# First taps of a pair's convolution, placed by an estimated landing time of their rows

## The chip, the cores and the metric

The kernel runs on one core of a Trainium2 chip. The metric is the device time of one execution in microseconds (us); the figure for the kernel before is the median of three runs.

## The reference

Two layers on `x` (8 batches, 4096 tokens, 192 channels). First a causal convolution over tokens with 7 taps; the taps are a softmax over the 7 weights of each of 8 heads, and a head has 24 channels. Then an MLP mixer:

```python
x_unf = x_pad[:, idx, :].reshape(B, S, K, H, group)
out = np.einsum('hk,bskhg->bshg', w, x_unf)          # the convolution
...
h = np.maximum(xt @ w_tok1, 0.0) @ w_tok2            # mixing of tokens
u = x + h.transpose(0, 2, 1)
h2 = np.maximum(u @ w_ch1, 0.0) @ w_ch2              # mixing of channels
return (u + h2).astype(np.float32)
```

## The kernel before, in words

**Groups and tiles.** The batches go in groups 0 to 4: two single batches (0 and 1), then three pairs (batches 2 and 3, 4 and 5, 6 and 7). The main loop goes over a group's 8 tiles of 512 tokens. Products keep float32's accuracy by splitting each operand into a high and a low part.

**One tile's steps on TensorE.** `mix2` (L899 to L901) finishes the token mixing. For a pair, DVE adds it to `u` (L914) and transposes it (L915), `blocks_sent` (L948) sends the blocks to their places with 16 small DMAs from SP and POOL, and `parted` makes the operands: `own_hi` on ACT (L961), `own_lo` on DVE (L963), and swapped copies in `other` (L966 on ACT, L968 by DMA). `channel1` is the first channel product (L999), in six steps of two results; from each result ACT makes `hh` (L1038) and DVE makes `hl` (L1039). `channel2` (L1073, L1074) and `channel2_halves` (L1056) are the second product, four parts `j` per tile; DVE adds each part's result into `osb` (L1079 and L1080, or L1062 and L1064). All results share `ps_x`, six PSUM buffers used in turn, so TensorE can be only a few results ahead of ACT and DVE.

**A turn.** In a pair's group, one `mix2` serves the tiles of both batches. It stands behind the second batch's `channel1`; that batch's `channel2` follows, with `parted` in its middle, and then `channel1` of the next tile's first batch. This text calls the place where that `channel1` begins a turn. The turns that matter here are in group 2: T1 begins at 607.00 us, T2 at 667.50, T3 at 735.80, T4 at 810.84 and T5 at 875.58 in the profiled execution.

**Work in the background.** While TensorE works on one group, a later group is convolved and its first token product is made (`stage1`). A pair is convolved in four blocks of 1024 tokens, q0 to q3 (`q2` in the code). For each half of the heads ("part") two DMAs on SP load the raw rows, 672 KB each (L639). The first tap of a head is a scaled copy on ACT (L649), which starts `xc`; the other six are multiply-adds on DVE into `xc` (L651). Finished blocks are stored to DRAM (`xcd`, L682, on POOL) and split for the product (`xhl`, ACT L734 and DVE L738).

**What sets the order.** The instructions are written out once, in Python, by a planner. `Background` keeps two running times in nanoseconds, `pe` and `dve`: what TensorE and DVE have been given so far. `fg` adds foreground work and then fills in background items while `dve` is not too far ahead of `pe`. An item can have a gate; a first tap's gate (`loaded`) is a time, and the tap is placed when `pe` has come to it. Each engine then runs its own instructions strictly in the order written, and waits in place for operands.

**Keeping loads back.** From before the `channel1` of a pair's second batch until `blocks_sent` is done, `bg.hold()` collects loads of raw rows and stores of `xcd`; `release` issues them right behind the 16 small DMAs. In the kernel before, a pair's load is marked, when it is issued, with `max(pe, dve)`; a first tap becomes due 6 us after that (10 us for q0).

Of the kernel before, what the change touches and what calls it, by code (L numbers as in the profile page):

```python
# [22 lines left out]
class Item:  # L23
# [6 lines left out]
    def __init__(self, fn, cost=0.0, lag=0.0, pe=0.0, gate=None, tag=None, eager=False):  # L30
        self.fn, self.cost, self.lag, self.pe, self.gate, self.tag = fn, cost, lag, pe, gate, tag
        self.eager = eager


class Background:
# [6 lines left out]
    def __init__(self):  # L42
        self.streams = []
        self.tiled = False
        self.pe = 0.0
        self.dve = 0.0
        self.held = None

    def transfer(self, fn):
        if self.held is None:  # L50
            fn()
        else:
            self.held.append(fn)
# [4 lines left out]

    def release(self):
        fns, self.held = self.held or [], None  # L60
        for fn in fns:
            fn()

    def add(self, items, lead=0.0, group=None):
        total = sum(it.cost for it in items) or 1.0
        self.streams.append(dict(items=items, total=total, done=0.0, free=self.pe, lead=lead, group=group))
# [65 lines left out]
def conv_mixer_kernel(ctx: ExitStack, tc: tile.TileContext, x, weight, w_tok1, w_tok2, w_ch1, w_ch2, out):  # L132
# [35 lines left out]
    bg = Background()  # L168
# [447 lines left out]
    def stage1(gi, pools):  # L616
        bs = GROUPS[gi]
        nb = len(bs)
# [11 lines left out]
        def load(q2, part):  # L630

            ds = slice(part * DH, (part + 1) * DH)
            raw = pools(part).tile([P, RB + HALO, nb, DH], F32, name=f"raw{part}")
            for i, b in enumerate(bs):

                at = (b * S + q2 * ST - HALO) * D + ds.start
                assert at >= 0
                src = bass.AP(tensor=x.tensor, offset=x.offset + at, ap=[[RB * D, P], [D, RB + HALO], [1, DH]])
                nc.sync.dma_start(out=raw[:, :, i, :], in_=src)  # L639
                if q2 == 0:  # L640
                    nc.gpsimd.memset(raw[0:1, 0:HALO, i, :], 0.0)
            return raw
# [13 lines left out]
        done = {}  # L656

        def mark(*key):
            done[key] = max(bg.pe, bg.dve)

        def begin(q2, part):
            def fn():
                states[q2]["raw", part] = load(q2, part)
                mark("load", q2, part)

            bg.transfer(fn)

# [92 lines left out]
        last_q = RB // MJ - 1  # L760
        def loaded(q2, part):
            at = done.get(("load", q2, part))
            return None if at is None or pools(q2 % 2) is None else at + (2e3 + 2e3 * nb if q2 else 10e3)

        def tap(q2, h, k):

            pace = PACE if gi == 1 and q2 + 1 < NS else 1.0
            it = Item(lambda: taps(q2, h, k), cost=2 * pace * (RB * nb * G / 0.96 + 130) if k else 0)
            if h % HH == 0 and k == 0:
                it.lag = 100  # L770

                def gate():
                    if h == 0 and q2 > 1 and ("split" if nb > 1 else "mixed", q2 - 2, last_q) not in done:
                        return None
                    return loaded(q2, h // HH)

                it.gate = gate
            convolving.append(it)
# [413 lines left out]
    for gi, bs in enumerate(GROUPS):  # L1192
        nb = len(bs)
# [109 lines left out]
```

## Time and profile before

| | us |
|---|---|
| median of 3 runs | 2048.83 (2048.3 to 2050.59) |
| the profiled execution's own time | 2047.31 |
| its span, first to last instruction | 2045.5 |
| TensorE busy | 2023.1 (99%) |
| DVE busy | 1453.1 (71%) |
| ACT, POOL busy | 761.7 (37%), 219.6 (11%) |

All readings below are of this one profiled execution. Its own time is 1.52 us under the median of the runs. In rows of the timeline, the first number is the start in us from the start of the span, the second the duration of the row's merged instructions; in brackets stands how long the engine was idle just before, and what ended that.

### The profile page before, as it was taken

How to read it: one execution, taken by the hardware profiler on the slowest of the kernel's cores; microseconds unless marked ns; L12 is line 12 of the kernel's file. 1: busy time of each engine (PE TensorE's matmuls, PEld its weight loads, DVE VectorE, ACT ScalarE, POOL GpSimd, SP SyncE). 2: the span in 40 equal slices, each digit the busy share in tenths (PEclk: the TensorE clock that was granted, in tenths of full speed). 3: DMA queues.
4: the chain of work that ended last, by engine and by line, in shares of the span. 5: the costliest groups of instructions: out<-in, count | busy, mean ns of one | idle time of the engine just before them, and what ended most of it. 6: DMA issues, size and time to landing. Idle time of an engine off the chain costs nothing.

```text
span 2045.5 us, 42015 instructions
## 1 busy us (share of the span) xinstructions
PE 2023.1 (99%) x17435; PEld 1858.9 (91%) x17435; DVE 1453.1 (71%) x2877; ACT 761.7 (37%) x1305; POOL 219.6 (11%) x383
## 2 busy tenths in 40 slices
PE   9999999999999989999999999999999999999999
PEld 9789999999988879999999999999999999999998
DVE  7899989999559978856985599545555555555554
ACT  4575534434332433333333334232323332333322
POOL 0100000000011011101111100111110011111110
PEclk9999999999999999999999999999999999999999
DMA  9845346554344475334645245533222333233310
GB/s 310 294 152 173 125 147 204 167 158 161 124 139 128 133 204 164 100 107 130 168 145 137 75 114 154 148 94 82 56 57 66 81 84 83 76 83 83 83 47 17
DMA packets 289230, 258.39 MB, mean 126 GB/s; under 512 B 209360, under 2 KB 238544, under 8 KB 289040
## 3 DMA queue, kind: packets, MB, share of 16 engines
q1 hardware_dynamic: 265120, 168.00, 28.9%
q0 software_dynamic: 23920, 87.71, 14.0%
q8 instruction: 138, 2.26, 0.5%
q14 instruction: 52, 0.43, 0.1%
HBM read 146.60 MB, written 71.30 MB: 107 GB/s over the span
## 4 chain that ended last, share of the span: by engine, by line
PE 89%; DVE 5%; DMA 3%; ACT 1%; SPq 1%; issue 0%; POOL 0%; ACTq 0%; POOLq 0%; DVEq 0%
PE ps_x L999 36%; PE ps_x L1073 16%; PE ps_x L1056 16%; PE ps_x L1074 7%; DVE xc L651 2%; PE ps_x L899 2%; PE ps_a L754 2%; PE ps_a L755 2%; PE ps_a L756 2%; PE ps_x L901 1%; PE ps_x L900 1%; DVE hl L1039 1%; DMA raw<-in_x_dram 1%; PE ps_a L444 1%; DMA dec_raw<-in_moe_w_tok_dram 1%; PE ps_x L896 1%
## 5 line engine op out<-in xcount | busy, mean ns | idle before, releaser
L1038 ACT ACTIVATE hh<-ps_x 128x512 fp32r<-128x512 f32 x756 | 410.6, 596 | 750.9 <-PE ps_x L999 750.9
L1039 DVE SCALAR_TENSOR_TENSOR hl<-ps_x,hh 128x512 fp32r<-128x512 f32 x756 | 484.3, 685 | 196.3 <-ACT hh L1038 195.3
L1073 PE MATMUL ps_x<-w,hh 128*128 128x384 f32 x1872 | 538.3, 359 | 0.1
L1074 PE MATMUL ps_x<-w,hl 128*128 128x192 f32 x1872 | 468.6, 250 | 0.0
L999 PE MATMUL ps_x<-other,w_hi 64*128 64x512 f32 x1728 | 452.7, 390 | 7.4 <-DVE osb L1080 7.2
L651 DVE SCALAR_TENSOR_TENSOR xc<-raw,cw,xc 128x384 f32<-128x384 f32 (+1 forms) x768 | 389.4, 561 | 24.7 <-ACT xc L649 24.7
L1074 PEld LDWEIGHTS ps_x<-w,hl 128*128 128x128 f32 x1872 | 357.4, 191 | 0.0
L999 PEld LDWEIGHTS ps_x<-other,w_hi 64*128 64x128 f32 x1728 | 314.7, 185 | 43.7 <-issue 8.3
L1073 PEld LDWEIGHTS ps_x<-w,hh 128*128 128x128 f32 x1872 | 351.5, 188 | 0.7 <-DVE hl L1039 0.7
L999 PE MATMUL ps_x<-own_hi,w_hi 64*128 64x512 f32 x1440 | 335.4, 394 | 5.7 <-DVE osb L1080 3.4
L1056 PE MATMUL ps_x<-w,hh 64*128 64x384 f32 x2304 | 330.2, 356 | 0.0
L999 PE MATMUL ps_x<-own_hi,w_lo 64*128 64x512 f32 x1440 | 326.2, 387 | 0.0
L999 PE MATMUL ps_x<-own_lo,w_hi 64*128 64x512 f32 x1440 | 326.1, 387 | 0.0
L1056 PE MATMUL ps_x<-w,hl 64*128 64x192 f32 x2304 | 291.7, 247 | 0.1
L999 PEld LDWEIGHTS ps_x<-own_hi,w_hi 64*128 64x128 f32 x1440 | 209.8, 184 | 40.5 <-issue 9.9
L999 PE MATMUL ps_x<-other,w_lo 64*128 64x512 f32 x864 | 242.8, 387 | 0.0
L999 PEld LDWEIGHTS ps_x<-own_hi,w_lo 64*128 64x128 f32 x1440 | 215.7, 184 | 27.5 <-DVE w_lo L204 0.5
L999 PEld LDWEIGHTS ps_x<-own_lo,w_hi 64*128 64x128 f32 x1440 | 215.8, 184 | 26.6
L1056 PEld LDWEIGHTS ps_x<-w,hl 64*128 64x128 f32 x2304 | 225.0, 188 | 1.8 <-DVE hl L1039 0.9
L1056 PEld LDWEIGHTS ps_x<-w,hh 64*128 64x128 f32 x2304 | 221.4, 184 | 0.9
L999 PEld LDWEIGHTS ps_x<-other,w_lo 64*128 64x128 f32 x864 | 159.4, 184 | 18.0
L1079 DVE TENSOR_TENSOR osb<-ps_x,u 128x192 f32<-128x192 f32 x156 | 55.4, 355 | 144.8 <-PE ps_x L1074 144.3
(143 smaller groups left out, 2151.6 us busy)
## 6 DMA issues: line engine op xcount, KB each, us to landing
raw<-in_x_dram SPq DMA_DIRECT2D x56, 672.0 KB, 7.2
t<-t2d SPq DMA_DIRECT2D x64, 512.0 KB, 5.4
out_dram<-osb POOLq DMA_DIRECT2D x63, 384.0 KB, 4.5
u<-xcd SPq DMA_DIRECT2D x62, 384.0 KB, 6.6
xcd<-xc POOLq DMA_DIRECT2D x28, 768.0 KB, 7.3
t<-t1p SPq DMA_DIRECT2D x32, 512.0 KB, 5.1
other<-own_hi SPq DMA_DIRECT2D x192, 48.0 KB, 2.1
other<-own_hi POOLq DMA_DIRECT2D x192, 48.0 KB, 2.0
```

The source lines that it names most:

```text
L651: nc.vector.scalar_tensor_tensor(out=dst, in0=src, scalar=cw[:, h, k:k + 1], in1=dst, op0=ALU.mult, op1=ALU.add)
L754: nc.tensor.matmul(out=ps, lhsT=wh, rhs=xh, start=a, stop=False)
L755: nc.tensor.matmul(out=ps, lhsT=wh, rhs=xl, start=False, stop=False)
L756: nc.tensor.matmul(out=ps, lhsT=wl, rhs=xh, start=False, stop=z)
L899: nc.tensor.matmul(out=ps[:, :n], lhsT=wh, rhs=hh, start=a, stop=False)
L999: nc.tensor.matmul(out=ps, lhsT=w1[w][rows, c, p * P:(p + 1) * P], rhs=t[h][v][rows, c], start=n == 0, stop=n == len(prods) - 1,)
L1038: nc.scalar.activation(out=h["hh", f], in_=ps, func=AF.Relu)
L1039: nc.vector.scalar_tensor_tensor(out=h["hl", f], in0=ps, scalar=0.0, in1=f32(h["hh", f]), op0=ALU.max, op1=ALU.subtract)
L1056: nc.tensor.matmul(out=ps[:, :m], lhsT=h[part, f][ks, ts], rhs=w2[ks, f, :m], start=n == 0 and part == "hh", stop=z and part == "hl",)
L1073: nc.tensor.matmul(out=ps[:, :2 * D], lhsT=h["hh", f][:, ts], rhs=w2[:, f, :], start=n == 0, stop=False)
L1074: nc.tensor.matmul(out=ps[:, :D], lhsT=h["hl", f][:, ts], rhs=w2[:, f, :D], start=False, stop=z)
L1079: nc.vector.tensor_tensor(out=rows(osb[:, j]), in0=rows(ps[:, :D]), in1=tokens(u, i)[:, j], op=ALU.add)
```

## The change

For a pair, a load no longer gets the time at which it is issued but an estimate of when it lands: 9 us after the later of now and the landing before it, so that loads are taken to land one by one. For loads that `release` issues, now is set 5 us later. The first tap is due at that estimate, with no further allowance. Single batches keep their rule.

```diff
@@ class Background
+        self.behind = 0.0
+        self.landing = 0.0
...
     def release(self):
         fns, self.held = self.held or [], None
+        self.behind = 5e3
         for fn in fns:
             fn()
+        self.behind = 0.0
+
+    def lands(self, took):
+        self.landing = max(max(self.pe, self.dve) + self.behind, self.landing) + took
+        return self.landing
@@ begin, in stage1
                 states[q2]["raw", part] = load(q2, part)
-                mark("load", q2, part)
+                if nb > 1:
+                    done["load", q2, part] = bg.lands(9e3)
+                else:
+                    mark("load", q2, part)
@@ loaded, in stage1
             at = done.get(("load", q2, part))
-            return None if at is None or pools(q2 % 2) is None else at + (2e3 + 2e3 * nb if q2 else 10e3)
+            if at is None or pools(q2 % 2) is None:
+                return None
+            return at if nb > 1 else at + (4e3 if q2 else 10e3)
```

No instruction is added or taken away on any engine; the same ones are written in another order. The order differs in two stretches only: a few taps of group 2 near 275 us, and the convolution of group 3 from T1 to T5 with what stands around it. From T5 on both orders are alike. In the changed kernel the line numbers are higher by 8 to 13 (L659 for L651, L976 for L963, L1092 and L1093 for L1079 and L1080, L1052 for L1039, L749 for L738, L657 for L649, L974 for L961, L979 for L966, L745 for L734, L1051 for L1038). Numbers behind names tell buffers apart.

DVE at T1, from `own_lo` to the first `hl`; `raw0_6694` holds the rows of block q0. Before:

```order
L963 TENSOR_TENSOR own_lo_6776<-other_6677,own_hi_6775 128x512 x3
L1079 TENSOR_TENSOR osb_6639<-ps_x_6758,u_6078 128x192
L1080 TENSOR_TENSOR osb_6639<-ps_x_6758,osb_6639 128x192
L651 SCALAR_TENSOR_TENSOR xc0_6822<-raw0_6694,cw_70,xc0_6822 128x16x24 x4
L1079 TENSOR_TENSOR osb_6639<-ps_x_6797,u_6078 128x192
L1080 TENSOR_TENSOR osb_6639<-ps_x_6797,osb_6639 128x192
L651 SCALAR_TENSOR_TENSOR xc0_6822<-raw0_6694,cw_70,xc0_6822 128x16x24 x4
L1039 SCALAR_TENSOR_TENSOR hl0_6841<-ps_x_6846,hh0_6840 128x512
```

Now:

```order
L976 TENSOR_TENSOR own_lo_6776<-other_6677,own_hi_6775 128x512 x3
L1092 TENSOR_TENSOR osb_6639<-ps_x_6758,u_6078 128x192
L1093 TENSOR_TENSOR osb_6639<-ps_x_6758,osb_6639 128x192
L1092 TENSOR_TENSOR osb_6639<-ps_x_6797,u_6078 128x192
L1093 TENSOR_TENSOR osb_6639<-ps_x_6797,osb_6639 128x192
L1052 SCALAR_TENSOR_TENSOR hl0_6834<-ps_x_6839,hh0_6833 128x512
L1052 SCALAR_TENSOR_TENSOR hl0_6834<-ps_x_6840,hh0_6833 128x512
L659 SCALAR_TENSOR_TENSOR xc0_6889<-raw0_6694,cw_70,xc0_6889 128x16x24 x2
```

The eight taps that stood ahead of the first `hl` stand behind it now, in twos.

DVE at T3, from `own_lo` to the first `hl`; before, `raw0_8260` holds the rows of block q2, loaded at this turn:

```order
L963 TENSOR_TENSOR own_lo_8354<-other_8243,own_hi_8353 128x512 x3
L651 SCALAR_TENSOR_TENSOR xc0_8387<-raw0_8260,cw_70,xc0_8387 128x16x24 x4
L1079 TENSOR_TENSOR osb_8171<-ps_x_8330,u_6835 128x192
L1080 TENSOR_TENSOR osb_8171<-ps_x_8330,osb_8171 128x192
L651 SCALAR_TENSOR_TENSOR xc0_8387<-raw0_8260,cw_70,xc0_8387 128x16x24 x8
L1079 TENSOR_TENSOR osb_8171<-ps_x_8396,u_6835 128x192
L1080 TENSOR_TENSOR osb_8171<-ps_x_8396,osb_8171 128x192
L738 TENSOR_TENSOR xhl_8433<-xc1_7597,xhl_8433 128x768
L651 SCALAR_TENSOR_TENSOR xc0_8387<-raw0_8260,cw_70,xc0_8387 128x16x24 x2
L1039 SCALAR_TENSOR_TENSOR hl0_8457<-ps_x_8462,hh0_8456 128x512
```

Now `raw1_7649` holds rows of block q1, long loaded, and `raw0_8252` those of q2:

```order
L659 SCALAR_TENSOR_TENSOR xc1_7680<-raw1_7649,cw_70,xc1_7680 128x16x24 x2
L976 TENSOR_TENSOR own_lo_8343<-other_8235,own_hi_8342 128x512 x3
L659 SCALAR_TENSOR_TENSOR xc1_7680<-raw1_7649,cw_70,xc1_7680 128x16x24 x2
L1092 TENSOR_TENSOR osb_8161<-ps_x_8322,u_6828 128x192
L1093 TENSOR_TENSOR osb_8161<-ps_x_8322,osb_8161 128x192
L659 SCALAR_TENSOR_TENSOR xc1_7680<-raw1_7649,cw_70,xc1_7680 128x16x24 x4
L1092 TENSOR_TENSOR osb_8161<-ps_x_8380,u_6828 128x192
L1093 TENSOR_TENSOR osb_8161<-ps_x_8380,osb_8161 128x192
L659 SCALAR_TENSOR_TENSOR xc0_8465<-raw0_8252,cw_70,xc0_8465 128x16x24 x6
L1052 SCALAR_TENSOR_TENSOR hl0_8438<-ps_x_8443,hh0_8437 128x512
```

All taps ahead of the last `osb` are of the old block; those of the new block begin behind it. On ACT, the four first taps of q2 stood right behind the swapped copies (L966); now the first `xhl` of q1 (L745) stands between.

DVE at T4, from `own_lo` to the first `hl`; before, `raw0_8767` (block q3, loaded 35 us earlier):

```order
L651 SCALAR_TENSOR_TENSOR xc1_9200<-raw0_8767,cw_70,xc1_9200 128x16x24 x6
L963 TENSOR_TENSOR own_lo_9212<-other_9087,own_hi_9211 128x512 x3
L651 SCALAR_TENSOR_TENSOR xc1_9200<-raw0_8767,cw_70,xc1_9200 128x16x24 x2
L1079 TENSOR_TENSOR osb_9015<-ps_x_9168,u_7610 128x192
L1080 TENSOR_TENSOR osb_9015<-ps_x_9168,osb_9015 128x192
L651 SCALAR_TENSOR_TENSOR xc1_9200<-raw0_8767,cw_70,xc1_9200 128x16x24 x4
L738 TENSOR_TENSOR xhl_9258<-xc0_8387,xhl_9258 128x768
L1079 TENSOR_TENSOR osb_9015<-ps_x_9249,u_7610 128x192
L1080 TENSOR_TENSOR osb_9015<-ps_x_9249,osb_9015 128x192
L651 SCALAR_TENSOR_TENSOR xc1_9200<-raw0_8767,cw_70,xc1_9200 128x16x24 x4
L1039 SCALAR_TENSOR_TENSOR hl0_9291<-ps_x_9296,hh0_9290 128x512
```

Now `raw1_8423` is of block q2, and `raw0_9091` of q3, loaded at this turn:

```order
L976 TENSOR_TENSOR own_lo_9180<-other_9074,own_hi_9179 128x512 x3
L659 SCALAR_TENSOR_TENSOR xc0_8465<-raw1_8423,cw_70,xc0_8465 128x16x24 x2
L1092 TENSOR_TENSOR osb_9002<-ps_x_9161,u_7592 128x192
L1093 TENSOR_TENSOR osb_9002<-ps_x_9161,osb_9002 128x192
L659 SCALAR_TENSOR_TENSOR xc1_9255<-raw0_9091,cw_70,xc1_9255 128x16x24 x10
L1092 TENSOR_TENSOR osb_9002<-ps_x_9217,u_7592 128x192
L1093 TENSOR_TENSOR osb_9002<-ps_x_9217,osb_9002 128x192
L749 TENSOR_TENSOR xhl_9253<-xc0_8465,xhl_9253 128x768
L659 SCALAR_TENSOR_TENSOR xc1_9255<-raw0_9091,cw_70,xc1_9255 128x16x24 x2
L1052 SCALAR_TENSOR_TENSOR hl0_9288<-ps_x_9293,hh0_9287 128x512
```

Ten taps of the block whose rows are loaded at this turn stand ahead of the last `osb`.

On SP, the loads of q1 and q3 for the first half of the heads, which went out between turns, go out at `release` now; the other halves' loads follow once their buffer is free. On POOL, the `xcd` stores of q1 and q2 stood ahead of the swapped copies (L968) at T3 and T4; they stand behind them now, and the store of q0 stands between the two output stores after T2 instead of ahead of both.

## The prediction

> **What bounds the kernel now.** I read the page's busy shares and chain first, then the waits of TensorE, then the timeline around them.
>
> ```profile
> PE 2023.1 (99%) x17435; PEld 1858.9 (91%) x17435; DVE 1453.1 (71%) x2877; ACT 761.7 (37%) x1305; POOL 219.6 (11%) x383
> ...
> PE 89%; DVE 5%; DMA 3%; ACT 1%; SPq 1%; issue 0%; POOL 0%; ACTq 0%; POOLq 0%; DVEq 0%
> ```
>
> TensorE bounds the kernel, and the change gives it no instruction less. So it can gain only time in which TensorE stands, or passes matmuls more slowly than elsewhere. The largest of its own waits:
>
> ```profile
> PE ps_x L999 <- DVE osb L1080: 10.5, 4, 4.4
> ```
>
> Four waits, 10.5 us: `channel1` needs a `ps_x` buffer that DVE has not emptied, since DVE is late with `osb`. They lie at T1, T2 and T3. Here stand, from the timeline, for T1 to T4 the first matmul of `channel1`, those that follow a wait, and the first of the product behind (L1056).
>
> ```profile
> 607.00 0.49 PE L999 MATMUL ps_x<-own_hi,w_hi 64*128 64x512 f32 x1
> 613.07 0.47 PE L999 MATMUL ps_x<-other,w_hi 64*128 64x512 f32 x1 [1.44 <-DVE osb L1080]
> 622.76 0.33 PE L1056 MATMUL ps_x<-w,hh 64*128 64x384 f32 x1
> 667.50 0.50 PE L999 MATMUL ps_x<-own_hi,w_hi 64*128 64x512 f32 x1
> 673.55 0.47 PE L999 MATMUL ps_x<-other,w_hi 64*128 64x512 f32 x1 [1.32 <-DVE osb L1080]
> 682.85 0.33 PE L1056 MATMUL ps_x<-w,hh 64*128 64x384 f32 x1
> 735.80 0.50 PE L999 MATMUL ps_x<-own_hi,w_hi 64*128 64x512 f32 x1
> 743.54 0.47 PE L999 MATMUL ps_x<-own_hi,w_hi 64*128 64x512 f32 x1 [3.36 <-DVE osb L1080]
> 748.43 0.76 PE L999 MATMUL ps_x<-other,w_hi 64*128 64x512 f32 x1 [4.42 <-DVE osb L1080]
> 758.27 0.33 PE L1056 MATMUL ps_x<-w,hh 64*128 64x384 f32 x1
> 810.84 0.49 PE L999 MATMUL ps_x<-own_hi,w_hi 64*128 64x512 f32 x1
> 823.24 0.33 PE L1056 MATMUL ps_x<-w,hh 64*128 64x384 f32 x2
> ```
>
> T4 is undisturbed: 823.24 - 810.84 = 12.40 us, 2.07 for each of six steps. T1 took 15.76, T2 15.35, T3 22.47: 3.36, 2.95 and 10.07 too much, **16.38 us** in all. Of it 10.54 is the four waits, 5.84 slow passing.
>
> Why DVE is late is seen on DVE, ACT and the DMAs: T1's and T2's row, then T3.
>
> ```profile
> 610.05 2.21 DVE L651 SCALAR_TENSOR_TENSOR xc<-raw,cw,xc 128x384 f32<-128x384 f32 x4 [4.27 <-ACT xc L649]
> ...
> 670.54 2.20 DVE L651 SCALAR_TENSOR_TENSOR xc<-raw,cw,xc 128x384 f32<-128x384 f32 x4 [2.75 <-ACT xc L649]
> ...
> 727.19 1.90 DVE L963 TENSOR_TENSOR own_lo<-other,own_hi 128x512 fp32r<-128x512 f32 x3 [0.46 <-ACT own_hi L961]
> 740.52 2.21 DVE L651 SCALAR_TENSOR_TENSOR xc<-raw,cw,xc 128x384 f32<-128x384 f32 x4 [11.44 <-ACT xc L649]
> 742.65 0.35 DVE L1079 TENSOR_TENSOR osb<-ps_x,u 128x192 f32<-128x192 f32 x1
> 743.03 0.36 DVE L1080 TENSOR_TENSOR osb<-ps_x,osb 128x192 f32<-128x192 f32 x1
> 743.31 4.31 DVE L651 SCALAR_TENSOR_TENSOR xc<-raw,cw,xc 128x384 f32<-128x384 f32 x8
> 747.54 0.35 DVE L1079 TENSOR_TENSOR osb<-ps_x,u 128x192 f32<-128x192 f32 x1
> 747.92 0.36 DVE L1080 TENSOR_TENSOR osb<-ps_x,osb 128x192 f32<-128x192 f32 x1
> 748.20 0.95 DVE L738 TENSOR_TENSOR xhl<-xc,xhl 128x768 fp32r<-128x768 f32 x1
> 749.06 1.14 DVE L651 SCALAR_TENSOR_TENSOR xc<-raw,cw,xc 128x384 f32<-128x384 f32 x2
> ```
>
> ```profile
> 724.94 14.45 SPq L639 DMA_DIRECT2D raw<-in_x_dram  x4
> 739.88 2.13 ACT L649 ACTIVATE xc<-raw,cw 128x384 f32<-128x384 f32 x4 [8.79 <-DMA raw<-in_x_dram]
> ```
>
> At T3 the rows are asked for at 724.94, behind the release; ACT stands until 739.88, and DVE, whose next taps need ACT's first one, for 11.44 us, with two parts of `osb` queued behind. From start to start four taps take 2.12 us (740.52 to 742.65) and two 1.06, so 0.53 each; `osb` takes 0.67, `xhl` 0.86. How long the second load of a part takes, beside the `xcd` stores at T3 and T4 and without them at T2:
>
> ```profile
> raw<-in_x_dram SPq DMA_DIRECT2D x1, 672.0 KB, 14.5
> xcd<-xc POOLq DMA_DIRECT2D x2, 768.0 KB, 8.4
> ...
> raw<-in_x_dram SPq DMA_DIRECT2D x1, 672.0 KB, 16.2
> ...
> raw<-in_x_dram SPq DMA_DIRECT2D x1, 672.0 KB, 7.4
> ```
>
> In order: T3, T4, T2.
>
> **The change part by part.** The measure for all turns is T4, where DVE was just early enough:
>
> ```profile
> 814.71 1.28 DVE L1039 SCALAR_TENSOR_TENSOR hl<-ps_x,hh 128x512 fp32r<-128x512 f32 x2
> 815.91 0.95 DVE L738 TENSOR_TENSOR xhl<-xc,xhl 128x768 fp32r<-128x768 f32 x1
> ```
>
> The first two `hl` took 1.20 and were done at 815.91, 5.1 us behind the turn. The six buffers go round: step 3 (2 x 2.07 = 4.1 us behind the turn) needs those of the last two parts `j`, step 4 (+6.2) those of step 1. So the last `osb` must be done by +4.1 and the first `hl` pair by +6.2.
>
> *T1.* No tap stands ahead of the first `hl`. Eight taps (4.24 us) and the 4.27 of waiting leave that place; `osb` is ready when TensorE is; step 1 ends at +2.1, and with 0.6 for `hh` and 1.20 the pair is done at about +4. Behind it taps and `hl` alternate at 1.06 + 1.20 = 2.26 us against 2.07: late by 0.19 a step, about 1 us over five steps, covered by the 2 us left. Gain 3.36 (at least the 1.44 of the wait).
>
> *T2.* Ahead of the first `hl` stand taps of the old block only, so no load is waited for.
>
> ```profile
> 665.23 1.90 DVE L963 TENSOR_TENSOR own_lo<-other,own_hi 128x512 fp32r<-128x512 f32 x3 [2.21 <-ACT own_hi L961]
> ```
>
> Two more taps ahead of `own_lo` go into its 2.21 of waiting. Behind it (665.23 + 1.81) come `osb`, two taps and the last `osb`, done at 669.4 or +1.9; then four taps, 2.12, and the pair, 1.20: +5.2, under 6.2. Gain 2.95 (at least 1.32).
>
> *T3.* Two taps go ahead of `own_lo`, partly into the 0.46 of waiting. Then two taps, `osb`, four taps: 727.19 + 0.6 + 1.81 + 1.06 + 0.67 + 2.12 = 733.5, before the turn at 735.80. The last `osb` follows at about +0.8, then six taps (3.2) and the pair (1.2): +5.2. The six need q2's rows. With 7.4 us they land at about 732.8 and cost nothing; with 14.5 at 739.9, then 0.6 to DVE's start, 3.2 and 1.2: +9.1, a wait of 2.9. I take 7.4, as the `xcd` stores now stand behind the swapped copies and behind q1's last tap, at about 733. Gain 10.07 (7.2 to 10.07).
>
> *T4.* This turn gets worse. Ten of the new block's taps stand ahead of the last `osb`. The release came 10.9 us before the turn at T3 (724.94 to 735.80). With 0.4 us to the second issue and 7.4 to its landing, the rows are there 3.1 before the turn, DVE starts 2.4 before it (0.64 behind ACT, as at T3), ten taps (5.3) and `osb` (0.67) end at +3.6, in time, and `xhl` (0.86), two taps (1.06) and the pair (1.20) at +6.7: 0.5 us too late. With 16.2 the end is at +15.5 and the wait 9.3. I take 0.5 (0 to 9.3): the row of T2 is the nearest, since here too the stores come behind the swapped copies.
>
> *Between turns.* Whether DVE can hold all this is read by stretches, turn to turn:
>
> ```profile
> core 0: us, PE busy (x) PEld busy (x) DVE busy (x) ACT busy (x) POOL busy (x), PEclk, DMA share, GB/s
> 735.80:810.84 75.04, 67.26 (x577) 62.24 (x576) 64.22 (x125) 28.33 (x47) 8.39 (x14) 0.95 0.57 162
> 810.84:875.58 64.74, 64.74 (x578) 60.01 (x578) 52.48 (x101) 22.94 (x37) 8.40 (x14) 1.00 0.49 138
> ```
>
> From T3's `own_lo` to T4's the order now holds 52 taps where it held 54, and from T4 to T5 50 for 42. So DVE needs 64.22 - 1.1 = 63.2 us of 75.04 - 10.07 = 65.0, and 52.48 + 4.2 = 56.7 of 64.7. It fits, but the first stretch is 97% full. I charge 0.6 us (0 to 5.84, all of the slow passing again).
>
> *Queues.* On SP the halves' loads stand ahead of the next tile's operands, on POOL one output store behind two `xcd` stores. What they carry is next read tens of us later, which hides it; with that cover gone the price is the few us that a load stands in its queue. I take 0. The shift near 275 us puts two taps ahead of an `hl` pair: 1.06 us at most either way; 0.2.
>
> *Sum.* -16.38 + 0.5 + 0.6 + 0.2 = -15.1 against the profiled 2047.31: 2032.2. The median stands 1.52 above that execution, so **2033.7**.
>
> **A rule weighed.** In this stretch of T3 the clock column reads half:
>
> ```profile
> 745.40:752.20 6.80, 3.77 (x18) 3.27 (x20) 6.77 (x14) 0.01 (x1) 0.59 (x1) 0.50 1.02 340
> ```
>
> So 10.07 - 3.36 - 4.42 = 2.29 us of T3's excess is slow passing, mostly at the lower clock, and it leaves with the waits. The Trainium skill, "TensorE: Matmul & The Clock Gate", section "What's actually happening", says that one idle window of about 3.4 us halves TensorE's clock. The trace agrees at T3, with waits of 3.36 and 4.42 us. By the rule T4's 0.5 us costs only itself, and the sum stays 2033.7, as by the rows; a wait like that of rival one would bring the half clock along, and its price is given both ways.
>
> **The rivals.** *One: T4 takes T3's place.* If the second load there takes 16.2 us, the wait is 9.3: 2033.7 + 8.8 = 2042.5; with the half clock as at T3, 2.29 more, 2044.8. For it: T4's own row, and that the stores go out within 2 us of `own_lo`, while the load may be in flight. Against it: T2's row. The Trainium skill, "DMA: Bandwidth & Descriptors", section "Issuing engines are not separate DMA queues", says that DMAs of all queues interleave on the same 16 engines: by that, order on POOL protects nothing that is still in flight, which is this rival.
>
> *Two: DVE full.* Taps between the `hl` pairs (2.26 against 2.07) and a DVE at 97% keep the slow passing: 2033.7 + 5.84 = 2039.5. Against it: T4 before, where taps stood there and nothing was lost.
>
> *Three, the other side: the transposes come late.* Taps stand among the transposes ahead of `blocks_sent`. `own_lo` ended at 729.1, 6.7 us before T3, which is the cover. To be slower by 0.2%, 19.2 us must be lost at T3, T4 and T5, so each `blocks_sent` would have to be 13 us later. At T5 only two to six taps more stand there, 1 to 3 us. Price at that point: 2052.9.
>
> *Four: the order changes but not the loss.* If many taps ahead of the last `osb` are the cause and not the idle 11.44, T4 now has T3's row of work and takes its 10.07, and T1's and T2's gains go into the full stretch: about 2048.
>
> **How the numbers follow.** As planned 0.68; rival one 0.14, of which 0.05 with the half clock, at the edge of no change; rival two 0.10; three 0.04; four 0.04. The measurement tells about 0.2%, 4.1 us, from no change. Faster: 0.68 + 0.09 + 0.10 = 0.87; same 0.05 + 0.04 = 0.09; slower 0.04. The likeliest case alone gives 2031 to 2037. The low end is all new costs at 0 and the shift's 1.06 gained: 2048.83 - 16.38 - 1.06 = 2031.4, less half a us of spread, 2031.0. The high end takes in rival two and most of rival one without the half clock: 2043.0.
>
> **What would show it.** Right: no wait of L999 for `osb` over 1.5 us; DVE's 11.44 before its taps gone; `channel1` at T1 to T3 within 13 us; the clock at full through T3. Wrong: T4's `channel1` near 22 us behind an ACT wait for `raw`, or steps of `channel1` stretched at all four turns.

## The result, and the profile after

The changed kernel takes 2033.39 us (median of 4 runs, 2031.83 to 2034.48), beside 2048.57 for the kernel before (4 runs, 2048.0 to 2050.59): a ratio of 0.9924 (95% interval 0.9906 to 0.9941). The profiled execution took 2034.48 us, span 2032.7, so it stands 1.09 above its median; that of before stood below its own.

The busy shares, and TensorE's largest row of waits in `channel1`:

```profile
PE 2019.6 (99%) x17435; PEld 1857.9 (91%) x17435; DVE 1452.2 (71%) x2877; ACT 761.7 (37%) x1305; POOL 220.3 (11%) x383
...
PE ps_x L1012 <- DVE osb L1093: 0.9, 1, 0.9
```

The instructions are the same; TensorE is 3.5 us less busy, and of 10.5 us of waiting for `osb` 0.9 is left. From the timeline, `channel1`'s first matmul at T1 to T4 and the first of the product behind it (L1069):

```profile
608.44 0.49 PE L1012 MATMUL ps_x<-own_hi,w_hi 64*128 64x512 f32 x1
620.83 0.33 PE L1069 MATMUL ps_x<-w,hh 64*128 64x384 f32 x2
665.34 0.50 PE L1012 MATMUL ps_x<-own_hi,w_hi 64*128 64x512 f32 x1
678.09 0.33 PE L1069 MATMUL ps_x<-w,hh 64*128 64x384 f32 x1
730.65 0.50 PE L1012 MATMUL ps_x<-own_hi,w_hi 64*128 64x512 f32 x1
743.03 0.33 PE L1069 MATMUL ps_x<-w,hh 64*128 64x384 f32 x2
795.38 0.50 PE L1012 MATMUL ps_x<-own_hi,w_hi 64*128 64x512 f32 x1
800.87 0.46 PE L1012 MATMUL ps_x<-other,w_hi 64*128 64x512 f32 x1 [0.89 <-DVE osb L1093]
809.93 0.33 PE L1069 MATMUL ps_x<-w,hh 64*128 64x384 f32 x1
```

T1 takes 12.39 us (before 15.76), T2 12.75 (15.35), T3 12.38 (22.47). T4 takes 14.55 and was 12.40: the changed kernel lost something there. These rows show DVE, ACT and TensorE at T4, and how long the second load of a half took at T3 and then at T4:

```profile
794.68 5.38 DVE L659 SCALAR_TENSOR_TENSOR xc<-raw,cw,xc 128x384 f32<-128x384 f32 x10 [3.96 <-ACT xc L657]
799.98 0.35 DVE L1092 TENSOR_TENSOR osb<-ps_x,u 128x192 f32<-128x192 f32 x1
...
802.56 2.48 DVE L1052 SCALAR_TENSOR_TENSOR hl<-ps_x,hh 128x512 fp32r<-128x512 f32 x4
...
794.02 2.14 ACT L657 ACTIVATE xc<-raw,cw 128x384 f32<-128x384 f32 x4 [2.17 <-DMA raw<-in_x_dram]
...
802.77 0.39 PE L1012 MATMUL ps_x<-other,w_hi 64*128 64x512 f32 x1
803.30 0.50 PE L1012 MATMUL ps_x<-own_hi,w_hi 64*128 64x512 f32 x1
803.89 0.50 PE L1012 MATMUL ps_x<-other,w_hi 64*128 64x512 f32 x1
...
raw<-in_x_dram SPq DMA_DIRECT2D x1, 672.0 KB, 6.8
...
raw<-in_x_dram SPq DMA_DIRECT2D x1, 672.0 KB, 9.2
```

Ten taps of the new block, whose rows come at 793.9, stand ahead of the last `osb`. Behind them the first pair of `hl` is late too: the matmuls at 803.30 and 803.89 start as its two parts end. They come 0.53 and 0.60 us behind the matmul before them, where 0.11 is usual (12.38 us for 108 matmuls at T3). A matmul's record lasts 0.39 us or more, so most of such a short stand is counted as busy and not as a wait. At T1 of the kernel before, two matmuls stand in the same way, at 615.69 and 616.29, and the prediction put that down to slow passing.

The stretches from turn to turn (columns as in the prediction):

```profile
608.44:665.34 56.90, 56.90 (x529) 51.91 (x528) 50.27 (x100) 19.67 (x37) 8.79 (x16) 1.00 0.52 142
665.34:730.65 65.31, 65.25 (x577) 60.18 (x576) 61.04 (x119) 28.73 (x48) 10.10 (x17) 1.00 0.63 174
730.65:795.38 64.73, 64.73 (x579) 60.01 (x578) 58.24 (x113) 24.74 (x42) 9.05 (x15) 1.00 0.57 164
795.38:862.55 67.17, 66.04 (x578) 60.40 (x578) 56.65 (x110) 23.62 (x39) 8.39 (x14) 1.00 0.53 159
```

Together 254.11 us from T1 to T5, and 268.58 before (607.00 to 875.58): 14.47 less. The granted clock is full in all four.

### The profile page after: what moved, and what is told of

It is laid out like the page before. It is cut to its first block, busy times and chain, and to the rows that moved or that the text cites. A ratio compares the mean times of both kernels' runs of the same rounds, so it can differ in the third digit from the quotient of the medians.

```text
span 2032.7 us, 42017 instructions
## 1 busy us (share of the span) xinstructions
PE 2019.6 (99%) x17435; PEld 1857.9 (91%) x17435; DVE 1452.2 (71%) x2877; ACT 761.7 (37%) x1305; POOL 220.3 (11%) x383
## 4 chain that ended last, share of the span: by engine, by line
PE 88%; DVE 5%; DMA 4%; SPq 1%; ACT 1%; issue 1%; POOL 0%; DVEq 0%; ACTq 0%
PE ps_x L1012 36%; PE ps_x L1086 17%; PE ps_x L1069 15%; PE ps_x L1087 8%; PE ps_x L912 2%; PE ps_a L765 2%; DVE xc L659 2%; PE ps_a L767 2%; PE ps_a L766 2%; PE ps_x L914 2%; PE ps_x L913 2%; PE ps_x L909 1%; PE ps_x L945 1%; PE ps_a L761 1%; DMA dec_raw<-in_moe_w_ch_dram 1%; DVE hl L1052 1%
## 5 line engine op out<-in xcount | busy, mean ns | idle before, releaser
L1051 ACT ACTIVATE hh<-ps_x 128x512 fp32r<-128x512 f32 x756 | 410.9, 596 | 743.3 <-PE ps_x L1012 743.2
L1052 DVE SCALAR_TENSOR_TENSOR hl<-ps_x,hh 128x512 fp32r<-128x512 f32 x756 | 484.5, 685 | 198.0 <-ACT hh L1051 196.6
L659 DVE SCALAR_TENSOR_TENSOR xc<-raw,cw,xc 128x384 f32<-128x384 f32 (+1 forms) x768 | 389.2, 562 | 9.8 <-ACT xc L657 9.8
L1069 PE MATMUL ps_x<-w,hh 64*128 64x384 f32 x2304 | 329.8, 355 | 0.0
L1069 PE MATMUL ps_x<-w,hl 64*128 64x192 f32 x2304 | 294.0, 247 | 0.0
L1069 PEld LDWEIGHTS ps_x<-w,hl 64*128 64x128 f32 x2304 | 229.0, 188 | 1.1 <-DVE hl L1052 0.2
L1069 PEld LDWEIGHTS ps_x<-w,hh 64*128 64x128 f32 x2304 | 225.2, 184 | 0.9
L1092 DVE TENSOR_TENSOR osb<-ps_x,u 128x192 f32<-128x192 f32 x156 | 55.4, 355 | 144.3 <-PE ps_x L1087 143.7
```

Source lines behind the costliest of these rows:

```text
L659: nc.vector.scalar_tensor_tensor(out=dst, in0=src, scalar=cw[:, h, k:k + 1], in1=dst, op0=ALU.mult, op1=ALU.add)
L1051: nc.scalar.activation(out=h["hh", f], in_=ps, func=AF.Relu)
L1052: nc.vector.scalar_tensor_tensor(out=h["hl", f], in0=ps, scalar=0.0, in1=f32(h["hh", f]), op0=ALU.max, op1=ALU.subtract)
L1069: nc.tensor.matmul(out=ps[:, :m], lhsT=h[part, f][ks, ts], rhs=w2[ks, f, :m], start=n == 0 and part == "hh", stop=z and part == "hl",)
L1092: nc.vector.tensor_tensor(out=rows(osb[:, j]), in0=rows(ps[:, :D]), in1=tokens(u, i)[:, j], op=ALU.add)
```

## The experiments

Each was timed in turn with the kernel before on the same chip; ratios are to that, with their 95% intervals. The line numbers are each kernel's own. The diffs are cut to what matters, with `...` where lines are left out.

**How much of the diff acts.** This much is read from the written order, with no run. With the landing reckoned from the present time alone, not one by one, every engine's instructions come in the same order as in the changed kernel, so that rule does nothing here. The same holds if the 5 us are added at T1's release alone. So one number at one place carries the change. The next kernel takes it out:

```diff
-        self.behind = 5e3
+        self.behind = 0.0
```

> The changed kernel, with the 5 us for loads that the release issues set to 0; the rest of the estimate (9 us for a load, one by one, no allowance behind it) stays. TensorE, POOL and SP then have the order of the kernel before everywhere, and DVE and ACT have it at all turns; only two taps near 275 us stand as in the changed kernel. Theory (the order at T1 to T4 carries the gain): 2048.6 us within 1.5, with DVE's 11.44 us of waiting at T3 back. Rival (the shift near 275 us carries part of it): 2 us or more below 2048.6.

Measured: 2047.86 us, ratio 1.0 (0.9991 to 1.0009). T3's `channel1` takes 22.50 us, and TensorE's waits are back:

```profile
PE ps_x L1012 <- DVE osb L1093: 9.5, 4, 4.4
```

What stays of the diff in it (the shift near 275 us) is worth nothing that this can tell.

**Are late rows the cause?** The kernel before, its pair loads not kept back:

```diff
-            bg.transfer(fn)
...
+            if nb > 1:
+                fn()
+            else:
+                bg.transfer(fn)
```

> The kernel before, with one thing changed: a pair's raw loads go out as soon as they are written, and are not kept back to the release; TensorE, DVE and ACT have the same instructions in the same order. Theory (the turns lose because DVE stands in line behind taps whose rows are still on the way): DVE's waits of 4.27, 2.75 and 11.44 us ahead of its taps at T1 to T3 shrink to under 1 us and channel1 there takes 12.4 to 13 us; of the 16.38 us 10 to 16 are gained, so 2033 to 2039 us against 2048.6. Rival A (the number of taps ahead of the last osb is the cause, whether the rows are there or not): T3's channel1 stays over 18 us and the time within 4 us of 2048.6. Rival B (the loads now run into the 16 small transposing DMAs): the waits for raw go, but TensorE waits for own_hi or other at the turns instead, some us at each, and the time is 2045 to 2055.

Measured: 2038.06 us, ratio 0.9955 (0.9942 to 0.9967). T3 falls to 13.52 us and T1 to 13.22, both above the 13 that I had given, but T2 stays at 15.34. ACT's and DVE's rows at T2:

```profile
664.91 1.48 ACT L972 CAST other<-own_hi 64x1536 fp32r<-64x1536 f32 x1
666.29 1.47 ACT L972 CAST other<-own_lo 64x1536 fp32r<-64x1536 f32 x1
668.52 2.13 ACT L649 ACTIVATE xc<-raw,cw 128x384 f32<-128x384 f32 x4
...
669.17 2.20 DVE L651 SCALAR_TENSOR_TENSOR xc<-raw,cw,xc 128x384 f32<-128x384 f32 x4 [2.75 <-ACT xc L649]
```

DVE waits as long as before, though ACT waits for nothing: its first taps stand in line behind the two swapped copies and an `xhl`. So the theory holds in the main for T3, in part for T1, and not for T2. At T3 too DVE still waits 2.67 us behind the copies.

**ACT's line, by itself.** The kernel before; at T2 alone the two copies are written behind the next two first taps:

```diff
-            nc.scalar.copy(out=swapped[k][high], in_=f32(own[k][low]))
+            fn = lambda k=k: nc.scalar.copy(out=swapped[k][high], in_=f32(own[k][low]))
+            if bg.turns == TURN:
+                bg.copies.append(fn)
...
+            if k == 0:
+                bg.copied()
```

> The kernel before, with one thing changed at T2 alone: ACT makes the first two taps of the new block ahead of the two swapped copies instead of behind them. All other engines and queues keep their order. Theory (at T2 the rows have long landed, and DVE's 2.75 us are spent on ACT's line, where the first taps stand behind the copies): DVE's wait ahead of its taps at T2 falls under 0.5 us, channel1 there takes 12.4 to 13.3 us in place of 15.35, T1 and T3 stay, and the time is 2 to 3 us less than before. Rival (the rows, or the number of taps, set it): wait or channel1 at T2 within 0.7 us of before, time the same. Rival B (the copies come too late for channel1's later steps): DVE's wait gone, but a new wait of channel1 for other at T2.

Measured: 2046.60 us, ratio 0.9991 (0.9982 to 1.0).

```profile
665.46 1.12 ACT L659 ACTIVATE xc<-raw,cw 128x384 f32<-128x384 f32 x2
666.61 1.47 ACT L979 CAST other<-own_hi 64x1536 fp32r<-64x1536 f32 x1
...
666.29 2.19 DVE L661 SCALAR_TENSOR_TENSOR xc<-raw,cw,xc 128x384 f32<-128x384 f32 x4
...
666.44 0.50 PE L1016 MATMUL ps_x<-own_hi,w_hi 64*128 64x512 f32 x1
668.14 0.49 PE L1016 MATMUL ps_x<-other,w_hi 64*128 64x512 f32 x1 [1.20 <-ACT other L979]
680.31 0.33 PE L1073 MATMUL ps_x<-w,hh 64*128 64x384 f32 x1
```

DVE's 2.75 us are gone, so at T2 they were ACT's line. But rival B came too: `channel1` reads the copies from its start, and waits 1.20 for them. T2 takes 13.87 us instead of 15.35, more than the 13.3 that I had given at most; the whole time can hardly show 1.5. The changed kernel, which puts taps of the old block there, gets most of the rest too (12.75).

**The stores beside T3's load.** The kernel before, the `xcd` stores of a turn issued behind the swapped copies on POOL; only POOL's order differs:

```diff
-            bg.transfer(fn)
+            if nb > 1 and (bg.held is not None or bg.turning):
+                bg.stores.append(fn)
+            else:
+                bg.transfer(fn)
...
             nc.gpsimd.dma_start(out=f32(swapped[k][low]), in_=f32(own[k][high]))
+        bg.turning = False
+        bg.stored()
```

> The kernel before, with the xcd stores that fall to a turn issued behind the swapped copies on POOL; all other queues and engines keep their order. Theory (T3's second load takes 14.5 us because two xcd stores of 384 KB run beside it): the second load lands in 7 to 9 us, DVE's wait at T3 falls from 11.44 to 4 to 6 us, T3's channel1 from 22.5 to about 15 to 17, T1 and T2 stay as they are; 2041 to 2044 us against 2048.6. Rival (other traffic, the swapped copies and the loads themselves, sets the 14.5): load and wait stay over 12 and 9 us, the time within 2 us of 2048.6.

Measured: 2039.61 us, ratio 0.9959 (0.9946 to 0.9971). The second load at T3, and DVE behind it:

```profile
raw<-in_x_dram SPq DMA_DIRECT2D x1, 672.0 KB, 6.0
...
730.10 2.21 DVE L659 SCALAR_TENSOR_TENSOR xc<-raw,cw,xc 128x384 f32<-128x384 f32 x4 [2.67 <-ACT xc L657]
...
733.96 0.50 PE L1013 MATMUL ps_x<-own_hi,w_hi 64*128 64x512 f32 x1
747.31 0.73 PE L1070 MATMUL ps_x<-w,hh 64*128 64x384 f32 x2
```

The load takes 6.0 us instead of 14.5, and `channel1` 13.35 instead of 22.47, better than I expected: of T3's 10.07 us 9.1 hung on two stores (768 KB each, not the 384 of the expectation) ahead of two copies, with no tap moved. T4's second load falls too, from 16.2 us to 7.5. The 2.67 that DVE still waits is about T2's 2.75: ACT's copies end only at 729.4. T1 took 14.25 us in this execution and 14.23 in that of the run above, both with T1's taps as they were, where the kernel before took 15.76; the second load there took 6.0 and 5.9 us, and 7.4 before. So about 1.5 us of T1's loss differs between executions.

**The taps moved at T3, the stores not.** The changed kernel, its 5 us from T3 on only:

```diff
-        self.behind = 5e3
+        self.behind = 5e3 if self.turns > 2 else 0.0
```

> The changed kernel, with the 5 us for released loads set to 0 at T1 and T2 and kept from T3 on. The order at T1 and T2 is then that of the kernel before; at T3 ten taps of the new block stand between the last two osb and none ahead of them (before: four and eight), and two xcd stores still stand ahead of the swapped copies on POOL. Theory (T3's loss is the second load's 14 us beside the xcd stores, T1's and T2's the place of the first taps on ACT and DVE): T1 and T2 keep their 14 to 16 us of channel1, the second load at T3 takes 13 us or more, channel1 there still takes over 18 us, and the time is 2043 to 2049 us. Rival (moving the taps is enough at T3, whatever the stores do): T3's channel1 under 15 us, and 2039 to 2042.

Measured: 2046.36 us, ratio 0.999 (0.9981 to 0.9999); the profiled execution is the slowest of its runs. The load, ACT and DVE at T3, TensorE, and the stretch of `channel1`:

```profile
raw<-in_x_dram SPq DMA_DIRECT2D x1, 672.0 KB, 15.2
...
741.29 2.13 ACT L658 ACTIVATE xc<-raw,cw 128x384 f32<-128x384 f32 x4 [8.29 <-DMA raw<-in_x_dram]
...
741.94 5.38 DVE L660 SCALAR_TENSOR_TENSOR xc<-raw,cw,xc 128x384 f32<-128x384 f32 x10 [11.14 <-ACT xc L658]
...
748.13 0.76 PE L1013 MATMUL ps_x<-other,w_hi 64*128 64x512 f32 x1 [6.99 <-DVE osb L1094]
...
736.54:758.80 22.26, 15.27 (x108) 12.52 (x109) 16.70 (x30) 8.04 (x15) 0.59 (x1) 0.77 0.86 235
```

With the stores in front, the load takes 15.2 us and T3 22.26, and T1 and T2 15.47 each, all about as before: the theory holds. The changed kernel has both, later stores and none of the new taps ahead of T3's last `osb`. Its order of taps with the stores in front was not run, so what that order alone would gain is not shown.

**T4: the ten taps or their rows?** The changed kernel, loads not kept back, with the same order on TensorE, DVE and ACT:

```diff
-            bg.transfer(fn)
+            if nb > 1:
+                fn()
+            else:
+                bg.transfer(fn)
```

> The changed kernel, with the pair's raw loads issued as soon as they are written instead of at the release; TensorE, DVE and ACT keep their order, with ten of the new block's taps ahead of the last osb at T4. Theory (T4's loss is the load's 9.2 us): the load is issued earlier, DVE's wait of 3.96 us at T4 falls under 2 us, channel1 there takes 12.4 to 13.2 us, and the time is 2031 to 2032 us. Rival A (the ten taps are too many even with their rows there): T4's channel1 stays over 14 us, about 2033.4. Rival B (the loads run into the 16 small DMAs of blocks_sent and the turns wait for the transposed blocks): 2034 us or more.

Measured: 2031.17 us, ratio 0.9916 (0.9903 to 0.993).

```profile
790.25 5.38 DVE L659 SCALAR_TENSOR_TENSOR xc<-raw,cw,xc 128x384 f32<-128x384 f32 x10 [1.69 <-ACT xc L657]
...
793.52 0.50 PE L1015 MATMUL ps_x<-own_hi,w_hi 64*128 64x512 f32 x1
805.90 0.33 PE L1072 MATMUL ps_x<-w,hh 64*128 64x384 f32 x2
```

With its rows there, T4 takes 12.38 us with all ten taps ahead of the last `osb`. The late rows are the whole of T4's loss.

**What makes T4's load 9.2 us?** The changed kernel, the two stores behind T4's copies moved behind the next output store:

```diff
-            bg.transfer(fn)
+            if gi == 3 and q2 == 2:
+                bg.stores.append(fn)
+            else:
+                bg.transfer(fn)
...
         queue.dma_start(out=dst[:, js.start:js.stop], in_=osb[:, js.start:js.stop])
+        bg.stored()
```

> The changed kernel, with the two xcd stores that follow T4's swapped copies issued behind the next output store on POOL, so after T4's second load of raw rows has landed; all other engines and queues keep their order. Theory (these stores, which start 3.6 us before that load lands, make it 9.2 us where T3's takes 6.8): the load takes 6.5 to 7.7 us, DVE's wait there falls from 3.96 to 1.5 to 2.7 us, channel1 at T4 takes 12.4 to 13.2 us in place of 14.4, and the time is 2031 to 2032 us. Rival (the swapped copies and the other loads of that moment, which stay, make it 9.2): load over 8.7 us, channel1 at T4 over 14 us, about 2033.

Measured: 2033.28 us, ratio 0.9925 (0.9911 to 0.9939). The load:

```profile
raw<-in_x_dram SPq DMA_DIRECT2D x1, 672.0 KB, 8.8
```

Without an `xcd` store beside it, the load still takes 8.8 us, and T4 14.17: my theory fell. What makes it longer than T3's 6.8, with swapped copies and a load of `t` beside it at both turns, stays open.

**A later estimate, and an earlier one.** The changed kernel with other numbers for a load, 11 us as here, then 13 and 7:

```diff
-                    done["load", q2, part] = bg.lands(9e3)
+                    done["load", q2, part] = bg.lands(11e3)
```

> The changed kernel, with 11 us in place of 9 for a load's landing. At T4 the taps of the new block then begin behind the last osb, as they do at T3. Theory (T4 loses 2.17 us because ten of the new block's taps stand ahead of the last osb and their rows come 4 us late): T4's channel1 takes 12.4 to 13 us in place of 14.56, and the time is 2031 to 2032 us against the 2033.4 of the changed kernel. Rival A (the taps put off fill the stretch behind T4 and slow it): no better than 2033.4. Rival B (DVE then waits for the same rows ahead of the first hl pair and T4 keeps its loss): T4's channel1 over 14 us, 2033 to 2034.

> The changed kernel, with 13 us in place of 9 for a load's landing: the taps of a new block begin later still (behind the last osb at all of T1 to T4, and some of the old block's taps are left over for T5). Theory (any estimate that keeps new rows' taps behind the last osb is good, since DVE has room behind the turns): as with 11 us, 2029 to 2031 us, channel1 at T1 to T5 12.4 to 13 us. Rival (taps that are put off pile up, and the stretch from T4 to T5 or T5 itself slows): over 2031.5 us, with a channel1 over 13.5 us at T5 or behind T4.

> The changed kernel, with 7 us in place of 9 for a load's landing. At T1 six taps of the new block stand ahead of the first hl, at T3 four of the old block and six of the new one ahead of the last osb (the changed kernel has the new ones behind it), at T4 twelve or so ahead of it, of a block loaded between the turns. Theory (what counts is whether new taps stand ahead of the last osb or the first hl while their rows or ACT are late): T1 loses 1 to 4 us and T3 0 to 5 against the changed kernel, T2 and T4 nothing, and the time is 2033 to 2041 us. Rival (the exact place of a few taps doesn't matter as long as the loads come one by one): within 1 us of the changed kernel's 2033 or below it.

With 11 us: 2029.59 us, ratio 0.9912 (0.9898 to 0.9925), under the 2031 to 2032 that I gave; T1 to T4 12.38 to 12.39 us each. At T4 DVE, then TensorE:

```profile
794.39 0.36 DVE L1092 TENSOR_TENSOR osb<-ps_x,u 128x192 f32<-128x192 f32 x1 [4.74 <-PE ps_x L1087]
...
794.28 0.50 PE L1012 MATMUL ps_x<-own_hi,w_hi 64*128 64x512 f32 x1
806.66 0.33 PE L1069 MATMUL ps_x<-w,hh 64*128 64x384 f32 x2
```

DVE waits for TensorE there now, and from T1 to T5 it takes 250.76 us (608.24 to 859.00), 3.35 less than the changed kernel. With 13 us: 2030.70, ratio 0.9917 (0.9903 to 0.993); T2 takes 13.20, the other turns and T5 12.4. Both theories hold in the main: T4's loss is gone, and no later turn pays for it. The intervals of the ratios overlap the changed kernel's, so that 11 beats 9 rests on the traces of the turns and on the two sets of times (2029.23 to 2030.30 against 2031.83 to 2034.48), taken on different occasions.

With 7 us: 2035.53, ratio 0.9935 (0.9923 to 0.9948). T1 takes 13.62, T3 and T4 12.38. At T3 six taps of the new block stand ahead of the last `osb` here, the stores behind the copies, and nothing is lost: with rows that come in time (the load takes 7.9 us) the place of these taps does not matter. The larger loss is in a place that I hadn't looked at, behind the turn that follows T5:

```profile
938.37 1.12 ACT L657 ACTIVATE xc<-raw,cw 128x384 f32<-128x384 f32 x2 [3.76 <-POOL raw L649]
...
939.02 1.15 DVE L659 SCALAR_TENSOR_TENSOR xc<-raw,cw,xc 128x384 f32<-128x384 f32 x2 [3.58 <-ACT xc L657]
```

First taps of group 4's first block come too early there, ahead of an `hl`, and from this `channel1` to the next it takes 30.69 us instead of 26.47. (ACT's wait ends with POOL, which writes zeros into these rows behind their load.) The time was in the range I gave, partly for another reason. Its interval overlaps the changed kernel's as well, so that 7 loses against 9 rests on these rows.

**The changed kernel once more**, beside those with 13 us and with free loads:

> The changed kernel itself, beside the other kernels of this set on one chip. Expected: 2033 us within 1.5, T4's channel1 14 to 15 us again, its second load of raw rows at T4 about 9 us. If the loss at T4 were chance of one execution, channel1 there would be under 13 us now.

Measured: 2032.76 us, ratio 0.9923 (0.9911 to 0.9936), T4 14.34 us and its second load 9.0: the loss is no chance of one execution.

## Why the prediction was right, and where it wasn't

The forecast was 2033.7 us, and faster; measured were 2033.39. The four signs named for being right all came: no wait of `channel1` for `osb` over 1.5 us, DVE's 11.44 gone, T1 to T3 within 13 us, and the clock at full through T3. Term by term, from the two profiled executions:

| | forecast, us | measured, us |
|---|---|---|
| T1 | -3.36 | 15.76 to 12.39: -3.37 |
| T2 | -2.95 | 15.35 to 12.75: -2.60 |
| T3 | -10.07 | 22.47 to 12.38: -10.09 |
| T4 | +0.5 | 12.40 to 14.55: +2.15 |
| between turns, T1 to T5 | +0.6 | -14.47 less the four above: -0.56 |
| the rest of the execution | +0.2 | 2047.31 to 2034.48, less -14.47: +1.64 |

The last row is mostly T1's start at 608.44 instead of 607.00. Among the other kernels here it lies anywhere from 606.85 to 608.35, with and without the shift near 275 us, so I read it as scatter. From median to median the change is -15.18, against -15.1 forecast.

**That it agrees to 0.3 us is in good part luck.** The measured terms add up to -12.83, not -15.1. The medians come nearer because the profiled execution of before stood 1.26 under its median and that of the changed kernel 1.09 above its own, where the forecast had added the same 1.52 to both. T1's term is luck in part as well: with its order unchanged T1 took 14.23 to 15.76 us in the executions here, so it gains 1.8 to 3.4.

**T4 is the term that was mis-sized.** "I take 0.5": the load was taken at T2's 7.4 us and took 9.2; rows landed 1.4 us ahead of the turn and not 3.1, DVE's taps began 0.7 ahead and not 2.4, and that is the 1.7 by which the term is short. The way of the loss was the one written: the first `hl` pair ended about 8.4 us behind the turn (6.7 reckoned) where step 4 needed it by 6.2, and T4 lost 2.15. I chose 7.4 because the stores come behind the copies; with the stores still later the load took 8.8, so they are not what makes it longer than 7.4. This is rival one, at a quarter of its price.

**Between turns** the lag that I charged shows once: the second batch's `channel1` at 634.46 took 12.88 us, where 12.36 is undisturbed, and in the changed kernel's other trace it took 12.36. But before there were losses between the turns too, which I hadn't counted, and part of them went; so the term came out with the other sign. This error hides more than half of T4's.

**T2's size was right, its reason wrong.** I took its wait with those for rows. The rows had long landed; free loads left the 2.75 us as they were, and moving ACT's copies took them away. Part of T1's and T3's waits is of this kind too: at T3 ACT itself stood 8.79 us, DVE 11.44. Nor was the size quite reached: 2.60 of the 2.95 went, and the 0.35 that stayed was not followed up.

**T3's step held as written**: the stores behind the copies, the load in 6.8 us. The stores alone gave 9.1 of the 10.07 us, new taps ahead of `osb` cost nothing behind a load of 7.9 (the run with 7 us), and moved taps beside a load of 15.2 gained nothing. Whether T3's own new order of taps would have been enough without the stores stays open; by the prediction's reckoning it would have left a wait of 2.9.

**Two rules beside the traces.** The load beside `xcd` stores takes 14.5 and 15.2 us at T3, and 6.0 with the stores behind: what stands on POOL slows what SP has issued. This agrees with the Trainium skill, "DMA: Bandwidth & Descriptors", section "Issuing engines are not separate DMA queues", by which DMAs of all queues share 16 engines. A wait of 6.99 us took the clock to 0.77 over T3's `channel1`, and its other 22.26 - 12.38 - 6.99 = 2.89 us are slow passing; beside waits of 0.89 (the changed kernel's T4) and 1.20 us (with ACT's line changed) it stayed at 1.00. That agrees with "TensorE: Matmul & The Clock Gate" of the Trainium skill, section "What's actually happening", which puts the window at about 3.4 us. In the kernel before, the clock stayed at 1.00 through T3's wait of 3.36 us (until 745.0) and read 0.50 only within the one of 4.42, so these traces don't say how long a wait it takes.

Rivals two, three and four are out: DVE held the taps, `channel1` starts no later at any turn behind T1, and the loss did not stay.

## What to carry to other kernels

When an engine with strict order waits at a boundary, ask of each instruction ahead of the critical one what it needs, back through the next engine's own line: here one engine's three waits had three causes, late rows, another engine's copies, and stores that slowed the load. An estimate that places work should err late while the engine has room behind the boundary: 11 and 13 us did as well as or better than 9, and 7 lost 1.2 us at T1 and 4.2 behind T5, more than the 2.2 that it won at T4. A small edit of a planner's number can act mostly through what else it moves, so compare every queue's order before costing it.

## What I had not expected of the hardware

The issue order of two 768 KB stores against two 384 KB copies on POOL changed a 672 KB load on SP from 14.5 to 6.0 us. Yet at T4 a load of the same size took 8.8 to 9.3 us in four executions of three kernels, with stores beside it or without, where T3's took 6.8 to 7.2. And T4 in the changed kernel lost 2.15 us of which the list of waits shows 0.89, with the clock at full: most of the rest is two short stands at the first `hl` pair, hidden in the busy time of the records. So a step that looks slow at full clock is best read by the starts of its matmuls.
